# Third half-sequence transposed by the DMA crossbar, with the output weights' load placed behind it

## The chip, the cores and the metric

One Trainium2 chip, one core of it. The metric is the device time of one execution in microseconds (us). Most executions of one kernel agree within about 1% here. In a trace PE is TensorE's matmuls, PEld its weight loads, DVE VectorE, ACT ScalarE, POOL GpSimd, SP SyncE; "SPq" and "POOLq" are their instruction queues. "Clock" is the TensorE clock that was granted, as a share of full speed; psum is the memory that TensorE writes its results to; "landing" is the end of a load, when those who wait for it may go on. L498 is line 498 of that kernel's file. The change takes five lines out above the feed-forward code, so before's L485, L498 and L507 (gate, value and output matmuls) are L480, L493 and L502 after.

## The reference

Attention over four sequences of 768 positions and eight heads (a local window of 96 and 8 global keys), then a feed-forward block with a gate:

```python
scores = scale * q @ k.T + bias            # kept: first 8 keys, or the last 96
a = softmax(scores)
x = (a @ v)                                # to (3072, 512)
out = (np.maximum(x @ w_gate, 0) * (x @ w_val)) @ w_out
```

## The kernel before

It works in eight half-sequences ("halves", numbered from 0) of 384 rows. TensorE does the feed-forward block of one half while the attention of the next is woven between its matmuls. q and k must be transposed before the score matmul. Halves 0 to 2 do it on TensorE (`piece_t`), halves 3 to 7 with the DMA crossbar (`early_pieces`):

```python
def piece_t(s, p):                      # on TensorE: six 128x128 transposes, then copies by VectorE
    tp = av_psum.tile([128, 512], FP32, name="av_ps") ...
    for i in range(2):
        for n in range(NN):
            nc.tensor.matmul(tp[:, i, n*128:(n+1)*128], lhsT=qk[:, i, n], rhs=ident,
                             is_transpose=True, ...)
    ...
def early_pieces(s):                    # by the crossbar
    out  = [piece_cast_k(s, p) for p in range(HP)]   # GpSimd: f32 -> bf16
    out += [piece_xk(s, n)     for n in range(NN)]   # SyncE: three DMA transposes of k
    out += [piece_cast_q(s, p) for p in range(HP)]   # GpSimd
    out += [piece_xq(s, n)     for n in range(NN)]   # SyncE: three DMA transposes of q
    out += [piece_order(s, p)  for p in range(HP)]   # GpSimd: keys into their windows
    # (cut: they are lists of closures, run in this order)
...
    load_w_group(2)                     # third of gate and value weights, GpSimd's DMA queue
    load_qk_after(2, nc.gpsimd, True)   # q, k of half 2: eight loads, SyncE's queue
    ...                                 # memsets
    load_v_globals(1)
    load_v_half(2)
    load_w(wo_sb, moe_w_out, 0, DM)     # "wo": output weights, 3 MB f32 -> 1.5 MB bf16
    for p in range(HP):
        piece_cast(2, p)
    spread_v_globals(1)                 # SyncE: six small copies, wait for load_v_globals
    ...
    weave(f1_1[0 : 4 * GW], [(0.1 * h, lambda h=h: mask(h)) for h in range(H)],
          [(0.5 + 0.14 * p, lambda p=p: piece_t(2, p)) for p in range(HP)])
    weave(f1_0[G[2]] + f1_1[G[2]] + f2_0 + f2_1,       # f2: the first users of wo
          spread(attention_pieces(2), 0.2, 0.9), [(0.25, lambda: load_qk_after(3, nc.vector))],
          ...)                          # (cut)
```

The instructions of each engine run in program order, as the traces show (after the change TensorE stands for 10.77 us before its first use of wo, with score matmuls of the same half still to come behind it). `load_qk_after` first writes one element of the load's target, so that the load waits for it.

The softmax here doesn't subtract the row's maximum and nothing guards it: scores larger than these inputs give would overflow.

Of the kernel before, what the change touches and what calls it, by code (L numbers as in the profile page):

```python
# [15 lines left out]
def kernel(  # L16
# [12 lines left out]
    nc = tc.nc  # L29

    B, H, S, D = q.shape
# [6 lines left out]
    HP = H // 2  # L38
# [67 lines left out]
    qTb = [const.tile([128, HP, 2, QH], BF16, name=f"qT{i}") for i in range(2)]  # L106
    kNb = [const.tile([128, HP, QH], BF16, name=f"kN{i}") for i in range(2)]
    qz = [const.tile([128, NN, HP, 2, 128], BF16, name=f"qz{i}") for i in range(2)]
# [4 lines left out]
    wo_sb = const.tile([128, N_FC, DM], BF16)  # L113
# [22 lines left out]
    def v_dst(b, r0, r1, j):  # L136
        t = vbuf[b % 2][r0:r1, j, D:]
        return t.rearrange("p (h z) -> p h z", z=2 * D)[:, :, 0:D]

    def load_v_globals(b):  # L140
        nc.gpsimd.dma_start(out=v_dst(b, 0, NG, 0),
                            in_=v[b, :, 0:NG, :].rearrange("h p d -> p h d"))

    def spread_v_globals(b, j0=1, j1=NT):
        for j in range(j0, j1):
            nc.sync.dma_start(out=v_dst(b, 0, NG, j), in_=v_dst(b, 0, NG, 0))
# [6 lines left out]
    def load_v(b, j, r0=0, r1=KT):  # L153
        n = min(r1, S - KT * j) - r0
        nc.gpsimd.dma_start(  # L155
            out=v_dst(b, NG + r0, NG + r0 + n, j),
            in_=v[b, :, KT * j + r0 : KT * j + r0 + n, :].rearrange("h p d -> p h d"))
# [5 lines left out]
    def load_v_half(s):  # L163
        b, half = divmod(s, 2)
        if half == 0 and s > 2:
            load_v_globals(b)
            spread_v_globals(b)
        for j in range(4) if half == 0 else range(4, NT):
            load_v(b, j)

    def load_w(dst, src, f0, f1):
        nc.gpsimd.dma_start(out=dst, in_=src[:, f0:f1].rearrange("(c p) f -> p c f", p=128))
# [5 lines left out]
    def load_qk_after(s, eng, by_pairs=False):  # L178

        qs_of[s] = stage.tile([128, H, NN * D], FP32, name="qs")  # L180
        ks_of[s] = stage.tile([128, H, NN * D], FP32, name="ks")
        step = 2 if by_pairs else H
        for t in (qs_of[s], ks_of[s]):
            eng.memset(t[0:1, 0:H:step, 0:1], 0.0)
        for h in range(0, H, step):
            load_qk(s, h, h + step)
# [44 lines left out]
    def mask(h):  # L231
        nc.scalar.activation(m_all[:, h], dd, AF.Exp, bias=0.0, scale=-slopes[h])
# [8 lines left out]
    def piece_cast(s, p):  # L241
        qk = cast_pool.tile([128, 2, NN, 2, D], BF16, name="qk")
        cast_of[s, p] = qk
        for i, src in ((1, ks_of[s]), (0, qs_of[s])):
            copy = nc.gpsimd.tensor_copy
            if s == 0:
                copy = (nc.vector.tensor_copy, nc.scalar.copy, nc.scalar.copy, nc.vector.tensor_copy)[p]
            elif s == 1 and p % 2 == 1:
                copy = (nc.scalar.copy, nc.vector.tensor_copy)[p // 2]
            copy(  # L250
                qk[:, i].rearrange("t n e d -> t e n d"),
                src[:, 2 * p : 2 * p + 2, :].rearrange("t e (n d) -> t e n d", n=NN))
# [20 lines left out]
    def piece_t(s, p):  # L273
        b, half = divmod(s, 2)
        kt = kT[b % 2][p]
        qk = cast_of[s, p]
        tp = av_psum.tile([128, 512], FP32, name="av_ps")
        tp = tp[:, 0:QH].bitcast(BF16).rearrange("d (i t) -> d i t", i=2)
        for i in range(2):
            for n in range(NN):  # L280
                nc.tensor.matmul(tp[:, i, n * 128 : (n + 1) * 128],  # L281
                                 lhsT=qk[:, i, n],
                                 rhs=ident, is_transpose=True,
                                 start=(i == 0 and n == 0), stop=(i == 1 and n == NN - 1))
        if s < 2:
            nc.vector.tensor_copy(qTb[s][:, p, 0, :], tp[:, 0, :])
        else:
            for e in range(2):
                r = slice(64 * e, 64 * e + 64)
                nc.vector.tensor_copy(qTb[s % 2][r, p, e, :], tp[r, 0, :])  # L290
        put_keys(nc.vector.tensor_copy, nc.vector.tensor_copy, kt, tp[:, 1, :], half)

    def piece_cast_k(s, p):
        nc.gpsimd.tensor_copy(  # L294
            kc[s % 2].rearrange("t n (h d) -> t h n d", d=D)[:, 2 * p : 2 * p + 2],
            ks_of[s][:, 2 * p : 2 * p + 2, :].rearrange("t e (n d) -> t e n d", n=NN))
# [20 lines left out]
    def early_pieces(s):  # L317
        out = [(0.0, lambda p=p: piece_cast_k(s, p)) for p in range(HP)]
        out += [(0.0, lambda n=n: piece_xk(s, n)) for n in range(NN)]
        out += [(0.0, lambda p=p: piece_cast_q(s, p)) for p in range(HP)]  # L320
        out += [(0.0, lambda n=n: piece_xq(s, n)) for n in range(NN)]
        out += [(0.0, lambda p=p: piece_order(s, p)) for p in range(HP)]
        return out
# [120 lines left out]
    def attention_pieces(s, fill=()):  # L444
        T = lambda p: [(0.34, lambda: piece_t(s, p))]
        QK = lambda p: [(0.18, lambda g=g: piece_qk(s, p, g)) for g in range(3)]
        AW = lambda p: [(0.58, lambda: piece_av_wide(s, p))]
        C = lambda p: [(0.0, lambda: piece_cast(s, p))]
        BI = lambda p, *gs: [(0.2, lambda g=g: piece_bias(s, p, g)) for g in gs]
        SC = lambda p, *gs: [(0.2, lambda g=g: piece_score(s, p, g)) for g in gs]  # L450
        X = lambda *fs: [(0.0, f) for f in fs]
        if s == 0:
            return (C(0) + X(lambda: load_v_globals(0), lambda: load_v(0, 0), lambda: load_v(0, 1),
                             lambda: load_v(0, 2), lambda: load_v(0, 3), lambda: load_w_group(0))
                    + C(1) + T(0) + BI(0, 0, 1) + C(2) + T(1) + SC(0, 0, 1) + BI(1, 0) + SC(1, 0) + C(3) + T(2)
                    + BI(1, 1) + SC(1, 1) + BI(2, 0) + T(3) + X(lambda: copy_v_globals(0, 1, 4))
                    + SC(2, 0) + BI(2, 1) + SC(2, 1)
                    + BI(3, 0) + SC(3, 0) + BI(3, 1) + SC(3, 1)
                    + AW(0) + AW(1) + X(lambda: load_qk_after(1, nc.vector, True)) + AW(2)
                    + AW(3) + X(second_pools, lambda: warm(4)))  # L460
        if s == 1:
            f = [[x] for x in fill]
            return (C(1) + T(0) + BI(0, 0, 1) + T(1) + SC(0, 0, 1) + f[0] + C(3) + BI(1, 0) + SC(1, 0)
                    + BI(1, 1) + SC(1, 1) + T(2) + f[1] + BI(2, 0) + SC(2, 0) + T(3) + BI(2, 1) + SC(2, 1)
                    + BI(3, 0) + SC(3, 0) + BI(3, 1) + SC(3, 1) + AW(0) + AW(1) + f[2] + AW(2) + f[3]
                    + AW(3) + f[4] + f[5])
        AV = lambda p: [(0.29, lambda e=e: piece_av(s, p, e)) for e in range(2)]
        g = QK(3)
        a = AV(2)
        return (QK(0) + QK(1) + AV(0) + QK(2) + AV(1) + g[0:1] + a[0:1] + g[1:2] + a[1:2] + g[2:3]  # L470
                + [(0.0, lambda: None)] * 2 + AV(3))
# [54 lines left out]
    def spread(items, first, last):  # L526

        n = len(items)
        return [(first + (i + 0.5) / n * (last - first), f) for i, (_, f) in enumerate(items)]
# [34 lines left out]
        f1_0[i][1]()  # L564
    other_pools()
    load_w_group(2)
    load_qk_after(2, nc.gpsimd, True)
    for p in range(HP):
        nc.gpsimd.memset(kT[1][p][:, 3, 32:128].bitcast(mybir.dt.uint32), 0)
        nc.gpsimd.memset(kT[1][p][:, 6, NG + 48 : 128].bitcast(mybir.dt.uint32), 0)  # L570
    nc.gpsimd.memset(vbuf[1][:, NT - 1, :].bitcast(mybir.dt.uint32), 0)
    for e in range(2):
        nc.gpsimd.memset(qTb[0][64 - 64 * e : 128 - 64 * e, :, e, :].bitcast(mybir.dt.uint32), 0)
    for j in range(NT):
        fill_ones(nc.gpsimd, 1, j)
    load_v_globals(1)
    load_v_half(2)
    load_w(wo_sb, moe_w_out, 0, DM)
    for p in range(HP):
        piece_cast(2, p)  # L580
    spread_v_globals(1)
    for i in range(2):
        nc.gpsimd.memset(qz[1 - i].rearrange("t n p e z -> t (n p e z)").bitcast(mybir.dt.uint32), 0)
    e3 = early_pieces(3)
    ck, xk, cq, xq, od = e3[0:HP], e3[HP : HP + NN], e3[HP + NN : 2 * HP + NN], e3[2 * HP + NN : -HP], e3[-HP:]
    weave(f1_1[0 : 4 * GW],
          [(0.1 * h, lambda h=h: mask(h)) for h in range(H)],
          [(0.5 + 0.14 * p, lambda p=p: piece_t(2, p)) for p in range(HP)])
    weave(f1_0[G[2]] + f1_1[G[2]] + f2_0 + f2_1,
          spread(attention_pieces(2), 0.2, 0.9), [(0.25, lambda: load_qk_after(3, nc.vector))],  # L590
          spread(ck + cq, 0.4, 0.45), [(0.45, lambda: load_v_half(3))],
          spread(xk, 0.52, 0.56), spread(xq, 0.64, 0.68), spread(od, 0.93, 0.97),
          [(0.55 + 0.05 * j, lambda j=j: fill_ones(nc.vector, 0, j)) for j in range(NT)])
# [46 lines left out]
```

## Time and profile before

| | before |
|---|---|
| median, three runs | 255.19 us (254.42 to 256.15) |
| profiled run, span | 251.3 us, clock 1.0 |
| TensorE busy | 241.4 us, 96% |
| wo issued / landed / first used | 36.2 / about 56 / 63.45 us |

How to read it: TensorE is dense, so time is won by taking work out of its stream and lost by whatever makes it wait. The chain that ended last shows at the first use of wo that it has no wait (start us, length, what):

```profile
62.96 0.65 PE ff_ps L498 x4
63.61 1.29 PE ff_ps L507 x6
64.90 0.53 PE av_ps L397 x8
```

One matmul group follows the other; no DMA stands between the value matmuls (L498) and the first of wo (L507).

### The profile page before, as it was taken

How to read it: one execution, taken by the hardware profiler on the slowest of the kernel's cores; microseconds unless marked ns; L12 is line 12 of the kernel's file. 1: busy time of each engine (PE TensorE's matmuls, PEld its weight loads, DVE VectorE, ACT ScalarE, POOL GpSimd, SP SyncE). 2: the span in 40 equal slices, each digit the busy share in tenths (PEclk: the TensorE clock that was granted, in tenths of full speed). 3: DMA queues.
4: the chain of work that ended last, by engine and by line, in shares of the span. 5: the costliest groups of instructions: out<-in, count | busy, mean ns of one | idle time of the engine just before them, and what ended most of it. 6: DMA issues, size and time to landing. Idle time of an engine off the chain costs nothing.

```text
span 251.3 us, 4907 instructions
## 1 busy us (share of the span) xinstructions
PE 241.4 (96%) x1751; PEld 143.0 (57%) x1751; DVE 133.0 (53%) x341; ACT 157.1 (63%) x316; POOL 89.4 (36%) x211
## 2 busy tenths in 40 slices
PE   7889989999999999999999999999999999999993
PEld 3556755666555666556664566556655666556541
DVE  3645464875464657527662567427662557424410
ACT  5886755636676687557774687557774687553321
POOL 7908993600558338403527076203610000000000
PEclk9999999999999999999999999999999999999999
DMA  6999999981899996938478966738562100030012
GB/s 173 165 209 235 161 226 236 191 135 39 255 141 261 183 212 135 98 109 262 107 85 86 257 166 146 60 108 258 108 83 82 43 3 1 16 111 0 0 42 83
DMA packets 77559, 33.13 MB, mean 132 GB/s; under 512 B 53472, under 2 KB 74464, under 8 KB 77536
## 3 DMA queue, kind: packets, MB, share of 16 engines
q1 hardware_dynamic: 45680, 24.93, 37.8%
q0 software_dynamic: 31856, 7.91, 32.0%
q8 instruction: 13, 0.21, 0.4%
q14 instruction: 10, 0.08, 0.1%
HBM read 28.38 MB, written 6.29 MB: 138 GB/s over the span
## 4 chain that ended last, share of the span: by engine, by line
PE 76%; ACT 6%; DMA 6%; DVE 6%; issue 2%; POOL 1%; SPq 1%; ACTq 0%; DVEq 0%; POOLq 0%
PE ff_ps L507 25%; PE ff_ps L498 20%; PE ff_ps L485 20%; PE av_ps L397 5%; PE qk_ps L369 4%; DMA wg<-in_moe_w_gate_dram 3%; DVE ht L500 3%; DVE xT L414 2%; DMA qs<-in_q_dram 2%; DMA ks<-in_k_dram 1%; ACT grelu L491 1%; ACT rcp L411 1%; ACT lnd L406 1%; ACT es L356 1%; PE av_ps L281 1%
## 5 line engine op out<-in xcount | busy, mean ns | idle before, releaser
L498 PE MATMUL ff_ps<-xT,wv 128*128 128x384 bf16 x384 | 77.7, 325 | 1.7 <-DVE grelu L489 0.8
L485 PE MATMUL ff_ps<-xT,wg 128*128 128x384 bf16 x384 | 77.8, 326 | 0.9 <-DMA wg<-in_moe_w_gate_dram 0.4
L500 DVE TENSOR_TENSOR ht<-ff_ps,grelu 128x384 bf16<-128x384 f32 x96 | 53.9, 562 | 25.4 <-PE ff_ps L498 20.4
L491 ACT ACTIVATE grelu<-ff_ps 128x384 bf16<-128x384 f32 x93 | 45.6, 490 | 34.5 <-PE ff_ps L485 19.1
L507 PE MATMUL ff_ps<-wo_sb,ht 128*128 128x512 bf16 x288 | 67.1, 379 | 0.0
L414 DVE TENSOR_TENSOR xT<-av_ps,rcp 64x384 bf16<-64x384 f32 x48 | 26.7, 555 | 45.1 <-ACT rcp L411 44.4
L485 PEld LDWEIGHTS <-wg 128*128 128x128 bf16 x384 | 36.2, 97 | 24.7 <-issue 1.7
L498 PEld LDWEIGHTS <-wv 128*128 128x128 bf16 x384 | 36.1, 97 | 24.4 <-issue 3.5
L381 DVE TENSOR_TENSOR es<-es,m_all 128x432 bf16<-128x432 bf16 (+5 forms) x108 | 33.4, 337 | 22.1 <-ACT es L372 21.6
L372 ACT ACTIVATE es<-qk_ps 128x432 bf16<-128x432 f32 (+2 forms) x72 | 37.9, 528 | 10.1 <-PE qk_ps L369 8.2
L507 PEld LDWEIGHTS <-ht 128*128 128x128 bf16 x288 | 27.0, 97 | 28.2
L294 POOL CAST kc<-ks 128x384 bf16<-128x384 f32 x20 | 10.2, 554 | 60.3 <-DMA ks<-in_k_dram 60.3
L406 ACT ACTIVATE lnd<-av_ps 64x384 f32<-64x384 f32 x48 | 23.3, 485 | 11.6 <-PE av_ps L397 11.0
L512 ACT COPY osb<-ff_ps 128x512 f32<-128x512 f32 x24 | 14.1, 586 | 25.4 <-PE ff_ps L507 24.5
L369 PE MATMUL qk_ps<-qT,kT 128*128 128x432 bf16 (+5 forms) x108 | 24.8, 286 | 0.0
L155 POOL DMA_DIRECT2D vbuf<-in_v_dram x28 | 24.5, 883 | 0.4 <-issue 0.4
L397 PEld LDWEIGHTS <-vbuf 128*128 128x128 bf16 x216 | 18.0, 98 | 7.4
L397 PE MATMUL av_ps<-es,vbuf 128*128 128x216 bf16 (+4 forms) x216 | 21.0, 226 | 0.0
L369 PEld LDWEIGHTS <-kT 128*128 128x128 bf16 x108 | 10.6, 98 | 7.6
L302 POOL CAST qz<-qs 128x192 bf16<-128x192 f32 x40 | 12.8, 370 | 2.8 <-DMA qs<-in_q_dram 2.6
L411 ACT ACTIVATE rcp<-lnd 128x384 f32<-128x384 f32 x24 | 12.5, 523 | 0.8
L356 ACT ACTIVATE es<-qk_ps 128x864 bf16<-128x864 f32 (+3 forms) x16 | 10.5, 709 | 3.6 <-PE qk_ps L351 3.5
(78 smaller groups left out, 145.1 us busy)
## 6 DMA issues: line engine op xcount, KB each, us to landing
out_dram<-osb SPq DMA_DIRECT2D x24, 256.0 KB
ks<-in_k_dram SPq DMA_DIRECT2D x5, 768.0 KB
qs<-in_q_dram SPq DMA_DIRECT2D x5, 768.0 KB
vbuf<-in_v_dram POOLq DMA_DIRECT2D x24, 120.0 KB, 4.7
ks<-in_k_dram SPq DMA_DIRECT2D x12, 192.0 KB
qs<-in_q_dram SPq DMA_DIRECT2D x12, 192.0 KB
wg<-in_moe_w_gate_dram POOLq DMA_DIRECT2D x3, 512.0 KB, 7.3
wv<-in_moe_w_val_dram POOLq DMA_DIRECT2D x3, 512.0 KB, 10.0
```

Source lines behind the costliest of these rows:

```text
L155: nc.gpsimd.dma_start(out=v_dst(b, NG + r0, NG + r0 + n, j), in_=v[b, :, KT * j + r0 : KT * j + r0 + n, :].rearrange("h p d -> p h d"))
L369: nc.tensor.matmul(ps[:, c : c + n_], lhsT=kt[:, j, :], rhs=qd[:, :, :, a : a + w], start=True, stop=True)
L372: nc.scalar.activation(es[:, 0:cols], ps[:, 0:cols], AF.Exp, bias=0.0, scale=scale)
L381: nc.vector.tensor_mul(e4, e4, mk)
L397: nc.tensor.matmul(av3[:, :, a : a + w], lhsT=vb[:, j, z0 : z0 + 128], rhs=es[:, c : c + NN * w].rearrange("k (n p) -> k n p", n=NN), star ...
L406: nc.scalar.activation(ln[o0 : o0 + 64], av[d0 : d0 + 64, 0:QH], AF.Ln, bias=0.0, scale=1.0)
L414: nc.vector.tensor_tensor(xT_of[s][r, p, :], av_of[s, p, e_][r, 0:QH], rc[r], op=ALU.mult)
L485: nc.tensor.matmul(psg[:, 0:QH], lhsT=w_of(wg, dc, fc), rhs=xT[:, dc, :], start=(dc == 0), stop=(dc == N_DC - 1))
L491: nc.scalar.activation(gr, psg[:, 0:QH], AF.Relu, bias=0.0, scale=1.0)
L498: nc.tensor.matmul(psv[:, 0:QH], lhsT=w_of(wv, dc, fc), rhs=xT[:, dc, :], start=(dc == 0), stop=(dc == N_DC - 1))
L500: nc.vector.tensor_tensor(ht[:, fc, :], psv[:, 0:QH], st[fc], op=ALU.mult)
L507: nc.tensor.matmul(ps2, lhsT=ht[:, fc, n * 128 : (n + 1) * 128], rhs=wo_sb[:, fc, :], start=(fc == 0), stop=(fc == N_FC - 1))
```

## The change

Its intent: take the 24 transposes of half 2 off TensorE, let the crossbar do them while no other large load is on the DMA engines, and for that hold wo back. The hold is one element: GpSimd copies a value that the first q transpose writes into wo's tile, so the load of wo must wait for that transpose.

```diff
-        if s < 2:
-            nc.vector.tensor_copy(qTb[s][:, p, 0, :], tp[:, 0, :])
-        else:
-            for e in range(2): ...
+        nc.vector.tensor_copy(qTb[s][:, p, 0, :], tp[:, 0, :])
...
-    load_qk_after(2, nc.gpsimd, True)
+    load_qk_after(2, nc.gpsimd)
...
     load_v_half(2)
+    spread_v_globals(1)
+    e2 = early_pieces(2)
+    for _, f in e2[:-HP]:
+        f()
+
+    nc.gpsimd.tensor_copy(wo_sb[0:1, 0, 0:1], qTb[0][0:1, HP - 1, 1, 127:128])
     load_w(wo_sb, moe_w_out, 0, DM)
-    for p in range(HP):
-        piece_cast(2, p)
-    spread_v_globals(1)
+    for _, f in e2[-HP:]:
+        f()
...
-          [(0.1 * h, lambda h=h: mask(h)) for h in range(H)],
-          [(0.5 + 0.14 * p, lambda p=p: piece_t(2, p)) for p in range(HP)])
+          [(0.1 * h, lambda h=h: mask(h)) for h in range(H)])
...
-          spread(attention_pieces(2), 0.2, 0.9), ...
+          spread(attention_pieces(2), 0.3, 0.9), ...
```

More of the change, by code (lines that the diff above doesn't have):

```diff
@@ L284, in piece_t @@
                                  start=(i == 0 and n == 0), stop=(i == 1 and n == NN - 1))
-        if s < 2:
-            nc.vector.tensor_copy(qTb[s][:, p, 0, :], tp[:, 0, :])
-        else:
-            for e in range(2):
-                r = slice(64 * e, 64 * e + 64)
-                nc.vector.tensor_copy(qTb[s % 2][r, p, e, :], tp[r, 0, :])
+        nc.vector.tensor_copy(qTb[s][:, p, 0, :], tp[:, 0, :])
         put_keys(nc.vector.tensor_copy, nc.vector.tensor_copy, kt, tp[:, 1, :], half)
@@ L571 @@
     nc.gpsimd.memset(vbuf[1][:, NT - 1, :].bitcast(mybir.dt.uint32), 0)
-    for e in range(2):
-        nc.gpsimd.memset(qTb[0][64 - 64 * e : 128 - 64 * e, :, e, :].bitcast(mybir.dt.uint32), 0)
+    nc.gpsimd.memset(qz[0].rearrange("t n p e z -> t (n p e z)").bitcast(mybir.dt.uint32), 0)
     for j in range(NT):
@@ L577 @@
     load_v_half(2)
-    load_w(wo_sb, moe_w_out, 0, DM)
-    for p in range(HP):
-        piece_cast(2, p)
-    spread_v_globals(1)
-    for i in range(2):
-        nc.gpsimd.memset(qz[1 - i].rearrange("t n p e z -> t (n p e z)").bitcast(mybir.dt.uint32), 0)
+    spread_v_globals(1)
[3 more added lines that the diff above has]
+    nc.gpsimd.tensor_copy(wo_sb[0:1, 0, 0:1], qTb[0][0:1, HP - 1, 1, 127:128])
+    load_w(wo_sb, moe_w_out, 0, DM)
+    for _, f in e2[-HP:]:
+        f()
+    nc.gpsimd.memset(qz[1].rearrange("t n p e z -> t (n p e z)").bitcast(mybir.dt.uint32), 0)
     e3 = early_pieces(3)
@@ L586 @@
     weave(f1_1[0 : 4 * GW],
-          [(0.1 * h, lambda h=h: mask(h)) for h in range(H)],
-          [(0.5 + 0.14 * p, lambda p=p: piece_t(2, p)) for p in range(HP)])
+          [(0.1 * h, lambda h=h: mask(h)) for h in range(H)])
     weave(f1_0[G[2]] + f1_1[G[2]] + f2_0 + f2_1,
-          spread(attention_pieces(2), 0.2, 0.9), [(0.25, lambda: load_qk_after(3, nc.vector))],
+          spread(attention_pieces(2), 0.3, 0.9), [(0.25, lambda: load_qk_after(3, nc.vector))],
           spread(ck + cq, 0.4, 0.45), [(0.45, lambda: load_v_half(3))],
```

## The prediction

> **What bounds the kernel now.** I read the page's busy shares first, then the chain that ended last, then the timelines of TensorE, GpSimd and SyncE between 24 and 92 us, then the DMA view in 2 us and 10 us stretches. The first line of the page:
>
> ```profile
> PE 241.4 (96%) x1751; PEld 143.0 (57%) x1751; DVE 133.0 (53%) x341; ACT 157.1 (63%) x316; POOL 89.4 (36%) x211
> ```
>
> TensorE is busy for 241.4 of 251.3 us, and 76% of the chain is PE, nearly all of it the feed-forward lines L485, L498 and L507. So the end moves by exactly what is taken out of TensorE's stream, or by what TensorE is made to wait for. The stretch that the change touches, from TensorE's timeline (start us, duration, line, operands):
>
> ```profile
> 46.75 0.81 PE L485 MATMUL ff_ps<-xT,wg 128*128 128x384 bf16 x4
> 47.40 0.50 PE L281 MATMUL av_ps<-ident,qk 128*128 128x128 bf16 x6
> 47.74 0.81 PE L498 MATMUL ff_ps<-xT,wv 128*128 128x384 bf16 x4
> 48.66 0.81 PE L485 MATMUL ff_ps<-xT,wg 128*128 128x384 bf16 x4
> 49.31 0.50 PE L281 MATMUL av_ps<-ident,qk 128*128 128x128 bf16 x6
> ...
> 62.80 0.81 PE L498 MATMUL ff_ps<-xT,wv 128*128 128x384 bf16 x4
> 63.45 1.46 PE L507 MATMUL ff_ps<-wo_sb,ht 128*128 128x512 bf16 x6
> ```
>
> The reader is to see three things. A group of four 384-wide matmuls starts 0.65 us after the one before it. A set of six transposes (L281) adds 0.33 to 0.34 us. After one of the sets the next group started 0.92 us later (47.74 to 48.66) rather than 0.65: VectorE was still copying transposed halves, so a psum tile came free 0.27 us late. And wo_sb is first read at 63.45.
>
> When wo and the other data come, from the DMA view of the stretch 30 to 40 us (size, us to landing) and the GpSimd and SyncE timelines:
>
> ```profile
> wo_sb<-in_moe_w_out_dram POOLq DMA_DIRECT2D x1, 1536.0 KB, 19.6
> vbuf<-in_v_dram POOLq DMA_DIRECT2D x1, 8.0 KB, 11.4
> ```
> ```profile
> 31.99 0.62 POOL L141 DMA_DIRECT2D vbuf<-in_v_dram  x1
> 32.60 3.63 POOL L155 DMA_DIRECT2D vbuf<-in_v_dram  x4
> 36.21 1.05 POOL L172 DMA_DIRECT2D wo_sb<-in_moe_w_out_dram  x1
> ```
> ```profile
> 43.45 4.82 SPq L146 DMA_DIRECT2D vbuf<-vbuf  x6
> 60.27 0.38 SPq L131 DMA_DIRECT2D ks<-in_k_dram  x1
> ```
>
> wo is issued at 36.21 and lands 19.6 us later, at about 56. That is 7.6 us before its first use: **it is hidden now, with little more than 7 us in hand**. The globals of v, 8 KB, take 11.4 us because they stand behind the third weight group in GpSimd's queue; they land at 43.4, and only then can SyncE issue the six copies that spread them, which take it until 48.3.
>
> How fast wo moves when it has the engines nearly alone, from the DMA view of 50 to 52 us (packets, MB, share):
>
> ```profile
> q0 software_dynamic: 382, 0.39, 117.0%
> ```
>
> 0.39 MB in 2 us is 195 GB/s of bf16, so the 1.57 MB of wo need **8.0 us**. In 30 to 40 us, beside a q and k load, the same queue moved 1.40 MB in 10 us: 140 GB/s.
>
> **What the Trainium skill says.** "DMA: Bandwidth & Descriptors", section "Queues, rings and completion order": each DMA engine takes its queue's descriptors in ring order and goes round-robin between queues. The trace agrees with both: the 8 KB load waits 11.4 us behind the weights, and the two queues share in 30 to 40 us. The same page, "Rules for kernel authors": a DMA transpose must come from SP or ACT, and one beside ordinary DMAs needs no extra order; so nothing but data and the queue order delays those added. "TensorE: Matmul & The Clock Gate", Part 4, gives some 275 ns for a TensorE transpose in a kernel; here a record is 219 ns, but pipelined, six cost 0.33 us, and I use that. The same page, Part 1: a whole idle window of about 3.4 us halves the clock until activity is seen again. Here the longest TensorE gap after the warm-up that I found is 0.8 us and the granted clock stays at 9 tenths or more, so no run shows it yet.
>
> **The change, part by part.**
>
> 1. Removed from TensorE: four sets of transposes, 4 x 0.335 = 1.34 us, all in a dense stretch, thus on the path. The one psum wait of 0.27 us goes too. **Gain 1.6 us.** VectorE loses 8 half copies of q (0.36 us each) and 12 key copies, and GpSimd loses 8 casts; both have idle time there, so these are worth nothing more.
>
> 2. Loads of q and k for the third half become two of 768 KB instead of eight. Same bytes, same queue. Now q's last part is cast at 45.41. With k ahead of q, k should land near 40.5 and q near 45.2.
>
> 3. The new chain on SyncE. It is in order: the spread of v's globals until 48.3 (above), then three k transposes, then three q transposes. Issues of the existing ones measure 1.26 us (k) and 1.31 us (q) at the median. So k until 48.3 + 3.8 = 52.1, the first q one until 53.4. The GpSimd casts are ready in time: k by 40.5 + 1.9 = 42.4, q by 45.2 + 2.8 = 48.0. For the fourth half-sequence's successor, the last k transpose was issued until 96.58 and GpSimd went on at 97.85 on its landing, 1.3 us later; I take 1.1 us here. **The first q transpose lands at about 54.5.**
>
> 4. wo is held for it. GpSimd copies one element of the result into wo_sb, then issues wo: 54.6 to 55.7 rather than 36.2. First bytes move near 56. The q and k of the fourth half are loaded from the place 0.25 in the second stretch; today at 60.27, after the change near 58.2, as TensorE gets there 1.6 us sooner and fewer score pieces stand before it. So wo moves alone for some 2.8 us, with two q transposes beside it (about 0.5 MB), and the other 1.07 MB at 140 GB/s take 7.6 us. **wo lands at about 66.4**, and at 64.7 if the other load costs it nothing.
>
> 5. When TensorE wants wo. The second stretch now starts at 52.0 (nine groups of 0.65 before the first score matmul at 57.87). After the change 52.0 - 1.6 = 50.4; sixteen groups, 10.4 us; and four score pieces instead of six before L507, because they are spread from 0.3 instead of 0.2: 4 x 0.17 = 0.7. So **61.5**. The score pieces moved behind are not saved, only later.
>
> 6. The wait: 66.4 - 61.5 = **4.9 us**, range 3.2 to 6. TensorE takes its stream in order, so everything behind it is late by as much, and the rest of the kernel is dense: nothing gives it back. A wait of that length may hold a whole idle window of 3.4 us, in some 4 of 10 phases ((4.9 - 3.4)/3.4); up to 3.4 us at half clock then cost up to 1.7. I put 0.3 in for it.
>
> Sum: 255.2 - 1.6 + 4.9 + 0.3 = **258.8 us**, 1.4% slower.
>
> **The rivals.** (a) *wo still comes in time*: then only the 1.6 us are left, 253.6 us. For it speaks that wo needs but 8 us alone. Against it, the sum of step 4 has wo issued 7 us before its use even at best, and issue, first byte and receipt take 2 of these. v's globals would have to land some 4 us sooner, yet the weight group ahead of them is untouched. (b) *The fence waits for all three q transposes*, if the order of the copy after the transposes is kept for the whole tile: 2.6 us more, 261.4 us and so slower by over 2%. The element chosen lies in the first third, which speaks for the design waiting for one. (c) *The crossbar data come late*: the first scores of the third half are wanted at about 58.9; the last q transpose is issued until 56.0 and lands near 57.3, the first keys are ordered by 56.7. It is close, but a small wait there only takes the place of a part of the wait for wo, and 258.8 stays. (d) *GpSimd becomes late for the fourth half*: it starts its key order after issuing wo and ends near 59.4, before that half's k can land, and TensorE wants its scores only at 82.84 now. No cost. (e) *The clock halves* during the wait: 260 to 261 us.
>
> **Range and chances.** From step 6, 1.6 less and 3.2 to 6 more give 256.8 to 259.6; the clock adds up to 1.7; the runs before scatter by 0.9 to either side. Leaving room for (a) below, the range is 254.6 to 262.0. Slower by over 2% means above 260.3: (b), (e) or a longer transpose chain, 0.25. Faster by over 2% means under 250.1, more than the TensorE work removed allows: 0.02. Within 2%: 0.73.
>
> **What would show it.** TensorE's timeline: no L281 after 30 us, groups 0.65 us apart up to 61.5, then one idle gap before the first L507, released by the DMA of wo. SyncE's: six transposes between 48 and 56. GpSimd's: one tiny copy released by the q transpose near 54.5, wo right behind it. The granted clock: a digit under 9 around 65 us if (e) is true. The prediction is wrong if no such gap is there (v's globals land sooner, or wo moves faster), or if it is over 6 us.

## The result and the profile after

The changed kernel took **267.68 us** (264.68 to 268.75, four runs; the longest counts as slow, being over 1.5% above the fastest, and is left out of the ratio), the kernel before of the same rounds 255.67 us. The ratio of the fast runs is **1.046** (95% interval 1.036 to 1.056). A ratio is the mean time of one kernel's fast runs over that of the other's of the same rounds, so it is not quite the ratio of the medians. The sign of the forecast was right; the loss is more than three times the 3.6 us forecast.

The timeline of TensorE, after (in brackets: idle time before, and what ended it):

```profile
62.20 0.81 PE L493 MATMUL ff_ps<-xT,wv 128*128 128x384 bf16 x4
62.85 0.35 PE L364 MATMUL qk_ps<-qT,kT 128*128 128x432 bf16 x1
73.97 0.61 PE L502 MATMUL ff_ps<-wo_sb,ht 128*128 128x512 bf16 x1 [10.77 <-DMA wo_sb<-in_moe_w_out_dram]
```

TensorE waits 10.77 us for wo, the only wait of more than a microsecond in its stream from 34 us on. The chain that ended last, after, shows what made wo late. Each line is the start, the length and what the chain ran through:

```profile
28.82 18.23 DMA qs<-in_q_dram
...
47.10 2.41 POOL qz L297 x8
49.52 0.68 SPq L146
...
50.29 1.31 SPq L300
...
51.65 1.74 SPq L300
...
53.45 1.26 SPq L300
...
54.82 2.77 DMA qT<-qz
...
58.26 15.67 DMA wo_sb<-in_moe_w_out_dram
```

Read it downwards: the casts of q end at 49.5, but SyncE is still spreading v's globals (L146) until 50.2. It then issues three k transposes (L300), and the first q transpose lands 2.77 us after its issue, at 57.6. Only now is wo issued, and it takes 15.67 us. Its issue is 22 us later than before.

Behind the wait TensorE is slow for a while. The stretches of the trace after (each row: the stretch and its length; busy time and instructions of PE, PEld, DVE, ACT and POOL; granted clock, DMA share, GB/s):

```profile
68.00:72.00 4.00, 0.00 (x0) 0.00 (x0) 0.00 (x0) 0.00 (x0) 0.00 (x0) 0.55 1.18 232
72.00:74.00 2.00, 0.03 (x1) 0.04 (x2) 0.00 (x0) 0.00 (x0) 1.10 (x3) 0.50 1.12 315
74.00:78.40 4.40, 4.18 (x11) 1.64 (x13) 0.73 (x2) 0.87 (x2) 3.28 (x11) 0.50 0.15 50
78.40:80.00 1.60, 1.60 (x11) 0.91 (x10) 0.28 (x2) 0.60 (x2) 1.60 (x3) 0.93 0.00 0
```

The clock went to half some 5 us into the wait and stayed there for the first 4.7 us of work (the last row, 0.93, still holds 0.2 us of it); less the gap of 0.2 us in it, this is 2.2 us lost.

The two profiled spans differ by 13.9 us. The wait is 10.8, the clock 2.2. A gap of 0.2 us right after it and a wait of 0.5 us for xT at 86.8 us come on top. TensorE's first common group after its early waits started at 38.48 rather than 36.93: 1.55 us that were lost before any changed work on TensorE. Less the 1.6 us of transposes and psum wait, this makes 13.7.

### The profile page after: what moved, and what is told of

Read it like the earlier page. It is cut to its first block, busy times and chain, and to the rows that moved or that the text cites.

```text
span 265.2 us, 4839 instructions
## 1 busy us (share of the span) xinstructions
PE 243.5 (92%) x1717; PEld 143.2 (54%) x1727; DVE 126.3 (48%) x321; ACT 157.3 (59%) x316; POOL 90.2 (34%) x226
## 4 chain that ended last, share of the span: by engine, by line
PE 68%; DMA 15%; ACT 6%; DVE 4%; SPq 2%; issue 1%; POOL 1%; ACTq 0%; POOLq 0%; DVEq 0%
PE ff_ps L502 24%; PE ff_ps L493 16%; PE ff_ps L480 16%; DMA qs<-in_q_dram 8%; DMA wo_sb<-in_moe_w_out_dram 6%; PE av_ps L392 5%; PE qk_ps L364 4%; DVE xT L409 2%; SPq L300 2%; ACT es L351 1%; ACT lnd L401 1%; DVE ht L495 1%; ACT rcp L406 1%; DMA qT<-qz 1%; PE qk_ps L346 1%
## 5 line engine op out<-in xcount | busy, mean ns | idle before, releaser
L502 PE MATMUL ff_ps<-wo_sb,ht 128*128 128x512 bf16 x279 | 68.1, 386 | 11.4 <-DMA wo_sb<-in_moe_w_out_dram 10.8
L495 DVE TENSOR_TENSOR ht<-ff_ps,grelu 128x384 bf16<-128x384 f32 x96 | 53.3, 555 | 31.1 <-PE ff_ps L493 26.0
L486 ACT ACTIVATE grelu<-ff_ps 128x384 bf16<-128x384 f32 x93 | 45.6, 490 | 34.3 <-DVE ht L495 15.6
L376 DVE TENSOR_TENSOR es<-es,m_all 128x432 bf16<-128x432 bf16 (+5 forms) x108 | 31.2, 318 | 35.0 <-ACT es L367 34.5
L289 POOL CAST kc<-ks 128x384 bf16<-128x384 f32 x24 | 11.5, 524 | 60.6 <-DMA ks<-in_k_dram 60.6
L297 POOL CAST qz<-qs 128x192 bf16<-128x192 f32 x48 | 14.7, 362 | 6.7 <-DMA qs<-in_q_dram 6.3
```

What stands on the lines that cost most here:

```text
L376: nc.vector.tensor_mul(e4, e4, mk)
L486: nc.scalar.activation(gr, psg[:, 0:QH], AF.Relu, bias=0.0, scale=1.0)
L495: nc.vector.tensor_tensor(ht[:, fc, :], psv[:, 0:QH], st[fc], op=ALU.mult)
L502: nc.tensor.matmul(ps2, lhsT=ht[:, fc, n * 128 : (n + 1) * 128], rhs=wo_sb[:, fc, :], start=(fc == 0), stop=(fc == N_FC - 1))
```

## The experiments

Theory: wo is late, for two reasons of like size (it starts late, and it shares the DMA engines), and nothing else of the change costs anything. Rivals: the crossbar itself costs time; the moved attention does; the half clock is of no account. Eleven kernels ran, all correct, beside the kernel before. Each table row gives wo's issue, its time to landing and TensorE's longest wait after 40 us in the profiled run.

| kernel | wo issued | to landing | longest wait, for | ratio to before (95%) |
|---|---|---|---|---|
| after | 58.3 | 15.7 | 10.8, wo | 1.046 (1.036 to 1.056) |
| e7 before, wo held | 60.3 | 16.1 | 12.6, wo | 1.060 (1.056 to 1.064) |
| e11 before, scores later | – | 19.1 | 0.6, VectorE | 1.001 (0.999 to 1.003) |
| e1 no hold | 48.3 | 14.4 | 6.9, qT | 1.032 (1.026 to 1.038) |
| e4 wo first | 38.2 | 21.3 | 3.0, qT | 1.008 (1.000 to 1.016) |
| e9 wo first, spread last | – | 22.2 | 1.7, xT; 1.3, qT | 1.012 (1.010 to 1.015) |
| e2 next load behind wo | 56.3 | 12.4 | 7.5, wo | 1.036 (1.030 to 1.043) |
| e3 spread last | 54.7 | 14.3 | 6.3, wo | 1.030 (1.023 to 1.036) |
| e8 e2 and e3 | 53.3 | 12.0 | 4.0, wo | 1.023 (1.019 to 1.028) |
| e6 fillers | 56.3 | 15.6 | 1.2 behind fillers, wo | 1.036 (1.033 to 1.040) |
| e5 wo first, scores 0.42 to 0.95 | – | 21.6 | 0.8, xT | 1.002 (0.999 to 1.004) |
| e10 wo first, scores 0.40 to 0.90 | – | 21.8 | 0.8, xT | 0.998 (0.996 to 1.000) |

(A dash: ahead of the casts, as in before and e4. e8's interval reaches below 2%, so that it is not clear whether it is slower by as much.)

### e7: the hold alone

The kernel before, TensorE transposes and all; only wo is held, for an element of the first score tile of half 2.

```diff
-    load_w(wo_sb, moe_w_out, 0, DM)
+    def late_wo():
+        nc.gpsimd.tensor_copy(wo_sb[0:1, 0, 0:1], es_of[2, 0, 0][0][0:1, 0:1])
+        load_w(wo_sb, moe_w_out, 0, DM)
...
+          [(0.235, late_wo)],          # in the second weave
```

> The kernel before, with its TensorE transposes, in which wo alone is held: one element of the first score tile of the third half (written near 59.5 us) is copied into wo_sb ahead of its load. Theory (late wo is the whole loss, the crossbar only sets how late): wo is issued near 60, beside the next q and k load, needs 14 to 16 us, lands at 74 to 76; TensorE waits 11 to 13 us at 63.5 and runs 2 us longer at half clock behind it; time 267 to 270 us. Rival (a good part of the loss is the crossbar's own, in other waits): time 259 to 264 us.

Measured: 269.57 us. Its TensorE timeline:

```profile
76.53 2.72 PE L507 MATMUL ff_ps<-wo_sb,ht 128*128 128x512 bf16 x6 [12.55 <-DMA wo_sb<-in_moe_w_out_dram]
```

A late wo by itself makes the whole loss and a little more, without one crossbar transpose added (a little more, as this hold opened later: wo was issued at 60.3 rather than 58.3 us). The theory holds; the rival that part of the loss is hidden elsewhere in the change falls.

### e11: the moved scores alone

```diff
-          spread(attention_pieces(2), 0.2, 0.9),      # in the kernel before
+          spread(attention_pieces(2), 0.3, 0.9),
```

> The kernel before with only the attention of the third half moved from 0.2 to 0.3, as the change has it. Theory (moving the scores costs nothing, so the loss of the changed kernel is not in this part): same within 0.5%. Rival (the shorter stretch makes ScalarE late): 1 us or more slower, with waits for xT between 70 and 83 us.

Measured: 254.88 us, ratio 1.001. As expected, this part is neutral.

### e1: the crossbar without the hold

```diff
-    nc.gpsimd.tensor_copy(wo_sb[0:1, 0, 0:1], qTb[0][0:1, HP - 1, 1, 127:128])
```

> The changed kernel without the one copied element: wo is issued by GpSimd right after the casts of q, near 49.6 us, and not behind the first q transpose (57.7). Theory (the hold makes wo late; the transposes themselves cost nothing on TensorE's path): wo has at most the transposes beside it, lands near 60 to 61 us, before its first use at 63.2; the 10.8 us wait and the half clock behind it (2.2 us) go, and the time is that of the kernel before less 1.6 us of transposes, 253 to 255 us. Rival (the crossbar loses to a large load beside it, which is why wo was held): wo is early but the transposes land late, TensorE waits several us at the first score matmul of the third half (near 60 us), and the time stays above 258 us.

Measured: 262.05 us, and here **the rival won**. wo was in time, but now TensorE waited for q. From the TensorE and SyncE timelines of this version:

```profile
65.65 0.52 PE L364 MATMUL qk_ps<-qT,kT 128*128 128x432 bf16 x1 [6.93 <-DMA qT<-qz]
```
```profile
48.40 5.30 SPq L300 DMA_TRANSPOSE kN<-kc  x3
53.81 10.09 SPq L304 DMA_TRANSPOSE qT<-qz  x3
```

The three q transposes took SyncE 10.09 us, where the changed kernel has 3.94. Why, the DMA view shows: first this version from 58 to 60 us (q0 carries wo, q1 the transposes: packets, MB, share), then the changed kernel from 56 to 58, where the transposes are alone:

```profile
q0 software_dynamic: 311, 0.32, 93.6%
q1 hardware_dynamic: 312, 0.07, 30.1%
```
```profile
q1 hardware_dynamic: 1695, 0.43, 93.8%
```

The two queues moved 311 and 312 packets: one each in turn (in e9, from 50 to 52 us, 305 and 305). But what the trace counts as a packet of wo is 1 KB (0.32 MB / 311) and one of a transpose a quarter of that (0.43 MB / 1695 = 254 bytes). So beside wo the crossbar got 0.07 MB in 2 us instead of 0.43, a sixth. So the thought behind the hold was right: the crossbar does lose beside a large load. Its price was put on wo instead.

### e4 and e9: wo first, no hold

e4 puts wo where the kernel before has it:

```diff
+    load_w(wo_sb, moe_w_out, 0, DM)
     spread_v_globals(1)
     e2 = early_pieces(2)
     for _, f in e2[:-HP]:
         f()
-    nc.gpsimd.tensor_copy(wo_sb[0:1, 0, 0:1], qTb[0][0:1, HP - 1, 1, 127:128])
-    load_w(wo_sb, moe_w_out, 0, DM)
```

> The changed kernel with wo issued where the kernel before issues it, ahead of the casts and transposes, and no hold: the crossbar part alone. Theory: wo lands near 56 to 58 us as before, six transposes run beside it from 50 to 59 us; if they are delayed by it they land at 60 to 61, a wait of up to 1.5 us at the first score matmul near 60.4; time 253 to 256 us, like the version without a hold or up to 1.5 us above it. Rival (transposes beside a large load are much slower): issue of a transpose well over 1.3 us each, the last q transpose lands after 64 us, time above 258 us.

Measured: 257.19 us, ratio 1.008. SyncE issued q transposes until 61.5, and TensorE waited 3.0 us for q, twice what I had allowed. That profiled run (259.09 us) counts as slow, being over 1.5% above this kernel's fastest, so I read only its order of events. How the DMA engines were used from 48 to 60 us, in the changed kernel and then in e10 (below; the same up to there as e4), with the same columns as above, of which the last two are DMA share and GB/s:

```profile
48.00:60.00 12.00, 12.00 (x76) 7.21 (x75) 5.09 (x12) 5.33 (x12) 3.43 (x11) 1.00 0.54 103
```
```profile
48.00:60.00 12.00, 12.00 (x76) 7.22 (x75) 5.14 (x12) 5.28 (x11) 1.27 (x5) 1.00 1.36 173
```

The hold leaves the engines half idle (share 0.54; the records of packets overlap, so that it can pass 1: q0 alone has 115% in a view of e8 below) at the very time in which wo could have come. With wo first the engines move 173 GB/s there instead of 103.

e9 then starts the transposes 5 us sooner, by spreading v's globals after them, and the scores at 0.38:

```diff
-    spread_v_globals(1)
     e2 = early_pieces(2)
     for _, f in e2[:-HP]:
         f()
+    spread_v_globals(1)
...
-          spread(attention_pieces(2), 0.3, 0.9),
+          spread(attention_pieces(2), 0.38, 0.93),
```

> Crossbar part, wo first and without a hold, v's globals spread after the transposes, attention of the third half over 0.38 to 0.93. Theory (transposes beside wo get one packet of 256 B for each of wo's 1 KB, so they finish only as wo does, about 57 to 60 us; starting them 5 us sooner makes them finish 1 to 2 us sooner): the last q transpose lands at 58 to 60.5, no wait at the first scores near 62, and with the attention less pressed than in the version from 0.42 to 0.95 the waits for xT of 1.0 us there shrink to under 0.5; time 253 to 254.5 us, ratio to before 0.993 to 1.0. Rival (the pressed attention costs what the transposes gain, wherever it is put): 254.5 to 256 us.

Measured: 257.88 us, ratio 1.012; a miss. SyncE's timeline:

```profile
45.13 4.84 SPq L300 DMA_TRANSPOSE kN<-kc  x3
50.08 11.46 SPq L304 DMA_TRANSPOSE qT<-qz  x3
```

They began 5 us sooner and ended at 61.5 all the same. That fits a fixed amount of DMA work shared in turns: with the engines busy throughout, its order doesn't change when all of it is done. That reading is argued from the two end times, not tested further. SyncE reached its later work (the spread, then the next q and k load at 66.3) some 5 us later than e4. Its time lies above the rival's range too: TensorE waited 1.3 us for q, then 1.7 and 1.4 us for xT and 0.7 for es. Before the first wait for xT ScalarE stood 1.44 us for an output store, one of those that SyncE issues; how much of the loss this makes was not tested.

### e2, e3 and e8: the two terms of the delay

e2 keeps the hold, but makes the next q and k load wait for wo:

```diff
-    load_qk_after(3, nc.vector)
+    load_qk_after(3, nc.gpsimd, after=wo_sb[0:1, 0, 0:1])   # copies this element, not a zero
```

> The changed kernel with the hold, but the next q and k load (1.57 MB, issued at 59.3 us, a microsecond after wo) held in its turn behind wo by one copied element. Theory (two terms of about equal size: wo issued late, and wo sharing the DMA engines with this load all the way): wo alone needs 8 us and some 2 us of start and receipt, lands at 68 to 69.5 instead of 74.0; the wait before the first use of wo falls from 10.8 to 5 to 6.5 us and the time by 4 to 6 us, to 261 to 263 us, if the later q and k do not make a wait of their own near 85 us. Rival (the rate of wo is its own and not the other load's doing): wo to landing stays near 15.7 us and the time at 267.

e3 leaves the hold and only moves the spread of v's globals behind the transposes (the first part of e9's diff).

> The changed kernel with the six copies of v's globals behind the six transposes in SyncE's order and not ahead of them. Theory (SyncE's order sets when the first q transpose is out: the copies hold it from 45.4 to 50.2): k transposes start near 43.5, the q ones at 49.5 when the casts of q are done, the first lands near 52, wo is issued near 52.5 instead of 58.3 and has 6 us without the next q and k load; it lands near 64 to 65. The wait before wo falls from 10.8 to 1 to 3 us, the clock stays up, time 255 to 258 us. Rival (the transposes wait for the DMA engines, busy with v until 47, not for SyncE): they end as late as before, wo is issued after 56 us, time above 264 us.

e8 has both edits.

> The changed kernel with both single edits at once: v's globals are spread after the transposes, and the next q and k load is held behind wo. Each alone took the wait for wo from 10.8 us to 7.5 and 6.3. Theory (the two terms add, as one is when wo starts and the other how fast it goes): wo is issued near 54.5, needs 11 to 12.4 us, lands at 65.5 to 67; the wait is 2.5 to 4 us; time 257 to 259.5 us. Rival (they are one thing: whichever is mended, the other takes over): wait above 5.5 us, time above 260.5 us.

Measured: 263.24, 261.56 and 259.89 us; waits of 7.5, 6.3 and 4.0 us. In e2 the wo load took 12.4 us instead of 15.7: sharing costs 3.3 us. In e3 it was issued at 54.7 instead of 58.3. Runs differ by up to 2 us before any changed work; counted from TensorE's first common group, wo is issued after 19.8 us in the changed kernel and in e2, and after 16.6 in e3 and 16.5 in e8: the place of the spread is worth 3.2 us. That phase is also why e2's wait missed its 5 to 6.5 us although wo landed at 68.6 as expected: TensorE came to it 2 us earlier than in the changed kernel. With both, it took 12.0 us and landed at 65.3. So both terms are real and they add roughly. e3 did less than I had expected: I had the fence open at 52, but the first q transpose, issued at 48.9, landed only near 54.1, 5.2 us after its issue where the changed kernel has 2.77; what slowed it is open. And e8 ended at the upper edge of its forecast (259.89 against 257 to 259.5):

```profile
65.35 2.18 PE L505 MATMUL ff_ps<-wo_sb,ht 128*128 128x512 bf16 x6 [3.95 <-DMA wo_sb<-in_moe_w_out_dram]
```

e8, where wo has no q and k load beside it, corrects a number: 12.0 us from issue to landing, of which 8.0 would be the bytes at 195 GB/s. The DMA view of e8 from 56 to 64 us:

```profile
q0 software_dynamic: 1453, 1.48, 115.0%
```

1.48 MB in 8 us is 185 GB/s, so the rate was right; but 2.7 us pass between the issue (53.3) and this stretch, and the tail ends at 65.3. About **4 us are start and end**, not rate.

### e6: the clock

```diff
+    def fillers():                      # 44 matmuls that nobody reads
+        t = av_psum.tile([128, 512], FP32, name="av_ps")
+        for _ in range(44):
+            nc.tensor.matmul(t, lhsT=wg[0][:, 0, 0:128], rhs=wg[0][:, 0, :], start=True, stop=True)
...
-    weave(f1_0[G[2]] + f1_1[G[2]] + f2_0 + f2_1,
+    weave(f1_0[G[2]] + f1_1[G[2]] + [(0.0, fillers)] + f2_0 + f2_1,
```

> The changed kernel with 44 matmuls of 512 columns that nobody reads (some 9.5 us) in TensorE's stream ahead of the first use of wo, to keep it busy during the 10.8 us wait. Theory (of the loss, 2.2 us are the half clock from 74.0 to 78.4 us that the idle time brought): the wait for wo itself stays where it ends, near 74 us, the granted clock stays whole, and the time falls by 1.5 to 2.5 us, to 264.5 to 266 us on runs where the changed kernel has 267. Rival (the clock costs nothing that matters): same time within 0.5 us, or longer by what the fillers stick out.

Measured: 263.30 us; ratio 1.036 against 1.046, one per cent (2.5 us) less than the changed kernel, though these two ratios are from different rounds and chips. The clean number is inside the profiles. From wo's first matmul to the end the changed kernel takes 265.2 - 73.97 = 191.2 us, this one 261.2 - 72.03 = 189.2. The stretch at half clock above, here:

```profile
74.00:78.40 4.40, 4.40 (x28) 2.29 (x26) 1.40 (x4) 3.04 (x7) 4.40 (x11) 1.00 0.33 91
```

The clock stays whole. So the idle time cost 2 us beyond itself. (The time fell by more than forecast, to 263.30 rather than 264.5 to 266, but the kernel before was 1.15 us faster in these rounds.) As a remedy it is worthless here: the wait that it hides is not needed at all.

How much idle time is needed for that can be read from the other traces. In e8, after the wait of 3.95 us above, the clock fell 0.6 us after work had begun again, and the whole slow stretch was work, so about half of it, 1.7 us, was lost:

```profile
65.95:69.37 3.42, 3.42 (x12) 1.38 (x10) 0.75 (x3) 0.87 (x2) 0.00 (x0) 0.50 0.63 179
```

In all seven traces with a wait of 3 us or more (the changed kernel, e1, e2, e3, e4, e7, e8) the clock stood at half for 3.41, 6.83, 10.24 or 13.65 us: whole multiples of 3.41. In e2 it fell 2.1 us after the last matmul, in e5 (below) behind a wait of 1.82 us; e10's wait of 1.72 us left it whole. So in these traces it was enough that TensorE idled for a little over half of a stretch of 3.41 us. This is inferred from the traces; no run varied the idle time alone.

### e5 and e10: a version without either wait

e5 is e4 with the attention of half 2 at 0.42 to 0.95, e10 with 0.40 to 0.90:

```diff
-          spread(attention_pieces(2), 0.3, 0.9),
+          spread(attention_pieces(2), 0.42, 0.95),    # e10: 0.4, 0.9
```

> The version with wo issued first and no hold, with the attention of the third half spread over 0.42 to 0.95 of the stretch and not 0.3 to 0.9. In the version without this TensorE waited 3.0 us at the first score matmul (until 63.2) for the last q transpose, and ran at half clock after it. Theory (the crossbar part costs only what its late landing makes TensorE wait, and wo needs no hold): the scores come after the landing, no wait over 0.5 us is left before 70 us, the 1.6 us of transposes are a net gain, time 252 to 254 us where the kernel before has 254.3. Rival (the attention pressed into a shorter stretch makes ScalarE late): a wait of 1 to 3 us for xT or a psum tile between 75 and 85 us, time 255 to 258 us.

> Crossbar part, wo first and without a hold, attention over 0.40 to 0.90: begun a little before that of the 0.42 to 0.95 version and done 1.3 us sooner. Theory (its end, not its start, made the wait of 0.8 us for xT at the next feed-forward): that wait goes, one of up to 0.6 us at the first scores may come, time 253.5 to 255 us, same as before within 0.5%. Rival (ScalarE can't do the exponentials of the half in so short a stretch): more waits between 72 and 82 us, time 255 to 257 us.

Measured: 254.74 us (1.002) and 254.36 us (0.998, interval 0.996 to 1.000): no faster than the kernel before. The wait for q is gone in both. In e10's TensorE timeline, after 40 us, two waits are left before the next half's feed-forward:

```profile
75.06 0.42 PE L392 MATMUL av_ps<-es,vbuf 128*128 128x216 bf16 x4 [0.81 <-DVE xT L409]
80.48 0.62 PE L392 MATMUL av_ps<-es,vbuf 128*128 128x144 bf16 x6 [0.31 <-DVE es L376]
```

These 1.1 us stand against the 1.6 us won. So it seems that the attention pressed into 0.5 of the stretch rather than 0.7 gives most of the gain back, and that the rival of e5 was right in kind, not in size. That is argued from single traces, not shown: e11's trace has waits of 0.56, 0.46 and 0.35 us that the kernel before hasn't, at an unchanged time. In e5 there is also a wait of 1.8 us for a weight group at 33 us and in e10 one of 1.7, where the kernel before has 0.43. It varies between the runs of the same code up to there (none is shown in e1, 0.89 in the changed kernel), so I take it as the scatter of the early loads. Whether the two large q and k loads make it more frequent stays open. In e5's profiled run the clock fell to half behind it for 3.41 us, and that run (256.19 us) lies 1.5 us above e5's median.

## Why the prediction was wrong

By its own steps:

- **Step 1, held.** No transpose is left on TensorE after 30 us and groups stand 0.65 us apart. The 1.6 us was not measured by a run of its own, but the traces show it: from TensorE's first common group (36.93 and 38.48) to the place of the first use of wo (63.45 before; after, 63.03, had there been no wait) it needs 26.52 us before and 24.55 after, and 0.35 of the difference are two score pieces moved behind. e10, with it, is 0.5 us or less below the kernel before, and its trace shows 1.1 us of new waits.
- **Step 2, held.** k was there at 41.5 and q at 47.1 (GpSimd's casts), 1 and 2 us later than said; neither delayed SyncE, which was spreading v's globals until 50.2.
- **Step 3, right in kind, short by 3.1 us.** The first q transpose landed at 57.6, not 54.5. v's globals came at 45.4 instead of 43.4 (+1.9, of which 1.55 are the late start of this whole run), the three k transposes took 4.42 instead of 3.8 us, and the first q one 2.77 instead of 2.4. The premise that "nothing but data and the queue order delays those added" did little harm here, with wo held, but it is wrong beside wo: 10.09 us for three q transposes in e1 against 3.94.
- **Step 4 is the one that failed: "wo lands at about 66.4".** It landed at 73.9. 3.7 us come from the issue at 58.26 instead of 54.6 (step 3, and 0.6 us more for copy and fence). 3.9 come from the way: 15.7 us instead of 11.8. I had counted 1.4 us to the first bytes, 0.5 MB in 2.8 us alone, 1.07 MB in 7.6 us at 140 GB/s, and nothing for the end. The first packets came at about 60.0, after 1.7 us. From there to 62.5 wo did have the engines alone: the next q and k load, issued at 59.31, moved its first packet only then. But it came slowly into its stride. Its queue from 60.0 to 62.5 us:

```profile
q0 software_dynamic: 213, 0.22, 92.9%
```

The other 1.35 MB then went beside that load, at 128 GB/s (1.28 MB from 62.75 to 72.75), and took until 73.9. So two terms were mis-sized. Start and end make some 4 us beyond the bytes (e8), where the sum held 1.4 (and 2 in rival (a)). And sharing costs 3.3 us (e2), where it held 2.1: 7.6 us less the 5.5 that 1.07 MB need at 195 GB/s. (By these figures the 64.7 us of step 4 should read 64.3, and the 3.2 us of step 6 2.8.)
- **Step 5, off by 1.7 us.** wo was wanted at 63.2, not 61.5, chiefly because this run was 1.55 us late before the changed stretch.
- **Step 6, right in kind: "4.9 us, range 3.2 to 6".** It was 10.8: 4.9, plus 7.6 for the landing, less 1.7 for the want. 1.55 us of both are the late start of this run; what counts is the issue (2.1) and the way (3.9). As said, nothing gave it back. **The clock, put in with 0.3 us, was 2.2** (e6: 2.0). Here the mechanism failed as well: the step asked for a whole idle window of 3.4 us, but e8's wait of 4.0 us and e4's of 3.0 brought the half clock too. The forecast wait of 4.9 us would have cost some 1.7 us by it, an estimate from e8.
- **Rivals.** (b) did not happen: the copy ran at 57.73, before SyncE had issued the third q transpose (until 58.76), so the fence waited for fewer than all three. (a) did not happen with the hold. (c) and (d) did not either: the first score matmul started at 60.39 with less than 0.1 us of waiting, and from 87 us on no wait over 0.22 us is shown. (e) did, with a wait twice as long.

In one sentence: the mechanism of the wait and its sign were right, but I gave the terms of wo's way too small values and reckoned too rarely with the half clock, and these errors all pointed the same way.

## What to carry to other kernels

Before holding one load behind another piece of work, add up its whole way: issue, start, bytes at the shared rate, end; and look at which load is issued next, as it will share most of the way (here from 62.5 us to the landing at 73.9). Small-packet DMA work (crossbar transposes) beside a large load was served packet by packet here (254 bytes against 1 KB) and got only a sixth of what it moved alone; but holding the large load moves the wait to whoever uses that load, so the question is which of the two has slack. Where TensorE is dense, an idle gap of 3 us or more cost its length here and 1.6 to 2.3 us of half clock besides.

## What the Trainium skill lacked or had wrong

- "DMA: Bandwidth & Descriptors", "Queues, rings and completion order", says that an engine takes queues in turn, packet by packet. The runs agree (311 packets to 312 in 2 us, e1, as the trace counts them). It lacks what this does to bytes: 0.32 MB to 0.07, as the one queue's packets are 1 KB and the other's 254 bytes.
- The same page, "Rules for kernel authors", says that a transpose next to ordinary DMAs needs nothing. That is about correct results, and all results here were correct; in time three transposes took SyncE 10.09 us beside wo and 3.94 without.
- The same page, "Anatomy of one DMA", gives a load issued by GpSimd (SWDGE) some 2.0 us of fixed cost. The casting load of wo had about 4 us beyond its bytes (e8: 12.0 us to landing, 8.0 at the rate of 195 GB/s), with only six small copies and two transposes beside it.
- "TensorE: Matmul & The Clock Gate", Part 1, lets the clock fall after at least one idle window of about 3.4 us. The length agrees: eight traces show half clock for 3.41 us or a whole multiple of it. That the window must be idle throughout does not: the clock fell 2.1 us after the last matmul in e2 and behind a wait of 1.82 us in e5.
